# Attention with mixed heads and two feed-forward layers: the values' product reads in storage order and writes PSUM in token order, and the first loads are reordered

## The chip, the cores and the metric

One Trainium2 chip, one core of it. The metric is device time in microseconds (us) of one execution. Five engines run their own instruction streams: TensorE (PE in the rows, with PEld for its weight loads), VectorE (DVE), ScalarE (ACT), GpSimd (POOL) and SyncE (SP), which here only issues DMAs. PSUM is where TensorE writes, SBUF is the working memory.

## What is computed

The inputs are q, k, v of shape (4, 12, 448, 64) in float32, two 12x12 matrices that mix the heads before and after the softmax, and two feed-forward layers of width 2048 on 1792 tokens of width 768, whose weights are float64.

```
scores = scale * q @ k^T                     # per batch and head, 448 x 448
scores = einsum('bhij,hg->bgij', scores, w_pre)
attn   = exp(scores - max) / (sum + 1e-9)
attn   = einsum('bhij,hg->bgij', attn, w_post)
x      = (attn @ v) as 1792 x 768
h = x @ w_in;   x = (h * cos(h)) @ w_out
h = x @ w_in2;  x = (relu(h) ** 2) @ w_out2
```

## The kernel before

The attention is made in 4 batches of 4 chunks of query rows (11, 12, 12 and 10 blocks of 10 rows each). For each chunk and each of six pairs of heads, `scores_ops` makes the products q k^T (L647), an engine copies them from PSUM to a tile `sh` (L655, L657), and SP moves each half with a DMA into a tile `t` that holds all 12 heads of a query row beside each other (L661). The loads of the next batch (`load_ops`, L515, and `value_loads`, L546) are laid out so that `turn_ops` (L570) can transpose q and k on TensorE.

For each pair of blocks, `pair_ops` mixes the heads on TensorE (L701, tile `m`), takes the row maximum (L709), exponentials (L717), the inverse sums, and then mixes the heads again on TensorE with the inverse sums in the moving operand (L747, tile `po`). `mixed` copies the result to `at` (L775, L777). In `at` the columns of one head are stored as (block, m), with five m to a block.

At the end of a chunk `value_ops` (L819) multiplies by v. Its two loops (L836, 128 rows and 64 columns of the array for each product, and L846, 64 rows and 64 columns) accumulate over the keys in one PSUM tile `av`. All operands are float32, and each such product stands in the trace as two records. The moving operand is read as

```
rhs=ao[:, 3 * r + jc, g, :w].rearrange("p (k m) -> p m k", m=HI)
```

so five runs of 10 to 12 elements, each with a step of five elements (20 bytes), and PSUM is written contiguously. ScalarE and VectorE then split the sums into two float16 parts in `x` (L859, L863).

Beside the attention, the sixteen pieces of w_in are loaded (L319), scaled, split into float16 parts and stored (L1810). After it the two layers run (L1145, L1245, L1541, L1738), with the weights of w_out, w_in2 and w_out2 being prepared beside the products.

The order on each engine is written before the run by the class `Plan` (L27): each operation has costs, dependences, buffers to acquire and a key. A model of the engines takes, at each moment, the ready operation with the smallest key. `KEYS` (L175) are the numbers that set these keys. What the planner holds as a cost or a dependence makes an order only; on the chip, waits come from data and buffers alone. All DMAs but those of the mixing matrices are issued by SP, in one order.

At the start SP issues the 24 loads of the first q and k (L533), the moves of the first chunk's scores (L661), the eight loads of v (L558), three pieces of w_in (L319) and the next batch's q (L535).

Of the kernel before, what the change touches and what calls it, by code (L numbers as in the profile page):

```python
# [9 lines left out]
F32 = mybir.dt.float32  # L10
# [16 lines left out]
class Plan:  # L27
# [3 lines left out]

    LAT, DMA_START, DMA_END = 170.0, 650.0, 1000.0
    ENGINES = ("PE", "ACT", "DVE", "POOL", "SP")
# [6 lines left out]

    def op(self, eng, cost, key, fn, deps=(), acq=(), rel=(), dma=None, seq=(), alone=False):
        o = {
            "alts": eng if isinstance(eng, dict) else {eng: cost},
            "key": (key, len(self.ops)), "fn": fn, "acq": tuple(acq), "rel": tuple(rel),
            "out": [], "next": [], "need": 0, "done": False, "n": len(self.ops), "dma": dma, "slot": {},
            "alone": alone,
        }
        for d in deps:
            if d is not None:
                self.after(o, d)  # L50
        for d in seq:
            d["next"].append(o)
            o["need"] += 1
        self.ops.append(o)
        return o

    def after(self, o, d):
# [3 lines left out]
    def run(self):  # L61
# [17 lines left out]
        while events:  # L79
# [12 lines left out]
            for e in self.ENGINES:  # L92
# [46 lines left out]
def tile_talking_heads_attention_two_ffn(  # L139
# [35 lines left out]
    KEYS = {  # L175
        "pm": (-2.47, -3.04, -3.36, -2.62),
        "po": (0.64, 0.12, 1.81, 1.95),
        "av": (-859.93, -0.46, -80.63, -319.88),
        "s": (-36.83, -2.97, -2.5, -3.27),
        "sd": (7.77, 0.78, 0.72, 0.91),  # L180
        "ld": (416.51, 281.47, 277.67),
        "t": (-175.97, -746.81, -11.1),
        "td": (16.48, -868.16, -740.81),
        "vl": (87.51, -100.51, -140.48),
        "v": (968.18, 285.48, -1312.57),
        "vd": (765.72, 172.63, -541.73),
        "t0": (306.0, -893.18),
        "f0": (-785.12, 21.82),
        "v0": (572.08, -1105.53),
        "w": (-55.5, 136.26, 197.7, 8.83, 82.8, -49.29, -83.67, 192.84, 126.4, 466.75, 452.07, -639.94, 926.33, 128.86, 649.7, 476.96),  # L190
        "w2": (102.69, -3359458.07),
        "wo": (2.01, 8.53),
    }
    SHB, EB, GB = 3, 5, 3
    SLOTS = (1, 2, 3, 1, 2, 3, 2, 3, 2, 3, 2, 3, 3, 3, 0, 0)
    WARM = (22, 6)
# [113 lines left out]
    def word_ops(src, rows, cols, nm, key, place, deps, acq=()):  # L310
# [43 lines left out]

        ld = add("SP", 475, key, load, deps, acq=acq, dma=3.85 * n)
        o = add({"POOL": 40 + 1.04 * n, "ACT": 190 + 0.83 * n}, 0, key, expo, [ld])
# [35 lines left out]
    def attention(r1, actx):  # L392
# [122 lines left out]
        def load_ops(b, key, step, seq=()):  # L515

            last, done = seq, []
            for hp in range(0, NP, step):
                outs = []
                for nm, src in (("q", q), ("k", k)):  # L520
                    parts = [(z, c) for z in range(2) for c in (range(NC4) if step > 1 else [None])]
                    for z, c in parts:
                        def go(e, nm=nm, src=src, z=z, c=c, hp=hp):
                            if (b, nm) not in raw:
                                raw[b, nm] = new_raw((b, nm)).rearrange(
                                    "p (h c x) -> p h c x", h=NP, c=NC4
                                )
                            to = raw[b, nm][:CP, hp : hp + step, :, 64 * z : 64 * z + 64]
                            hs = src[b, 2 * hp + z : 2 * (hp + step) : 2].rearrange(
                                "h (p c) d -> p h c d", c=NC4  # L530
                            )
                            if c is None:
                                SP.dma_start(out=to[:, 0], in_=hs[:, 0])  # L533
                            else:
                                SP.dma_start(out=to[:, :, c], in_=hs[:, :, c])  # L535
# [5 lines left out]
                        last = [o]  # L541
                        outs.append(o)
                done += [outs] * step
            return done, last

        def value_loads(b, key, seq=()):  # L546
# [9 lines left out]
            for p0, jc, t0, c, n in parts:  # L556
# [4 lines left out]

                o = add("SP", 570, key, go, acq=[] if outs else ["v"], dma=13.5 * n, seq=last)
                last = [o]
# [6 lines left out]
        def turn_ops(b, keys, loads):  # L570

            outs, last = [], None
            for hp in range(NP):
# [14 lines left out]
                def keep(e, hp=hp, box=box):  # L588
# [9 lines left out]
                outs.append(add(  # L598
                    {"ACT": 950, "DVE": 1060}, 0, keys[hp], keep, [last], rel=[("m", last)], alone=True
                ))  # L600
# [35 lines left out]
        def scores_ops(b, ch, hp, key, turned, before):  # L636
# [22 lines left out]
            def move(z):  # L659
# [6 lines left out]
                return go  # L666

            o = add(
                "PE", 760, key, mm, [turned[hp], before],
                acq=["m"] + (["t"] if hp == 0 else []), rel=[f"qk{hp}"] if ch == 3 else [],  # L670
            )
            l = add(
                {"ACT": 950, "DVE": 1060}, 0, key, copy, [o], acq=["sh"], rel=[("m", o)], alone=True
            )
            return o, [
                add("SP", 850, key, move(z), [l], rel=["sh"] * z, dma=10 * m) for z in range(2)
            ]
# [7 lines left out]
        def pair_ops(st, moved, before_pm, before_po):  # L685
# [84 lines left out]
            def mixed(e):  # L770
# [31 lines left out]
            )  # L802
            o = add("DVE", 1090 if n == 2 else 580, s + 0.1, row_max, [pm], alone=True)
            ex = add("ACT", 830 * n, s + 0.2, exps, [o], acq=["e"], rel=[("m", pm), "pm"])
            rc = add({"DVE": 80, "POOL": 230}, 0, s + 0.3, guard, [ex])
            rc = add("DVE", 140, s + 0.3, recip, [rc], alone=True)
            rc = add({"DVE": 190, "POOL": 350}, 0, s + 0.4, mixer, [rc, w4], acq=["g"])
            po = add(
# [3 lines left out]
            low = add(  # L812
                {"ACT": 890, "DVE": 1000} if n == 2 else {"ACT": 950, "DVE": 800}, 0,
                s + KEYS["po"][b] + 0.1, mixed, [po], acq=["at"] if st.blk[0] == 0 else [],
# [4 lines left out]
        def value_ops(b, ch, key, lows, vready, before):  # L819
# [4 lines left out]
            def mm(e):  # L824
# [36 lines left out]
            def lo(e):  # L861
# [6 lines left out]
            o = add(  # L868
                "PE", 4900, key, mm, [before] + lows + vready[0] + x_free[b], acq=["m"],
                rel=["at"] + (["v"] if ch == 3 else []),  # L870
            )
            h = add("ACT", 850, key + 0.1, hi, [o] + vready[1])
            x_fin[b].append(add("DVE", 1100, key + 0.15, lo, [h], rel=[("m", o)], alone=True))
            return o


        def spaced(nm, n):
            return [KEYS[nm][0] + KEYS[nm][1] * i for i in range(n)]
# [916 lines left out]
    for f in range(NF):  # L1795
# [9 lines left out]
        def write(w, o, n, f=f, i=i, box=box):  # L1805
# [8 lines left out]
            o = halves(w, get, o, n, key)  # L1814
            return add("SP", 475, key, store, [o], dma=1060, rel=[] if i else ["raw"])

# [45 lines left out]
```

## Time and profile before

| | us |
|---|---|
| median of 3 runs | 1453.8 |
| lowest and highest | 1444.34, 1456.33 |
| the profiled execution, device time | 1451.96 |
| its span in the trace | 1449.9 |
| attention, until the last values' product | 0 to 518 |
| TensorE busy over the span | 1336.8 |

The span runs from the first to the last instruction; 2.1 us of the device time lie outside it. Busy time counts an instruction as long as its record, and records of matmuls overlap.

### The profile page before, as it was taken

How to read it: one execution, taken by the hardware profiler on the slowest of the kernel's cores; microseconds unless marked ns; L12 is line 12 of the kernel's file. 1: busy time of each engine (PE TensorE's matmuls, PEld its weight loads, DVE VectorE, ACT ScalarE, POOL GpSimd, SP SyncE). 2: the span in 40 equal slices, each digit the busy share in tenths (PEclk: the TensorE clock that was granted, in tenths of full speed). 3: DMA queues.
4: the chain of work that ended last, by engine and by line, in shares of the span. 5: the costliest groups of instructions: out<-in, count | busy, mean ns of one | idle time of the engine just before them, and what ended most of it. 6: DMA issues, size and time to landing. Idle time of an engine off the chain costs nothing.

```text
span 1449.9 us, 35787 instructions
## 1 busy us (share of the span) xinstructions
PE 1336.8 (92%) x15255; PEld 880.1 (61%) x15255; DVE 895.8 (62%) x1647; ACT 677.3 (47%) x1271; POOL 387.2 (27%) x436
## 2 busy tenths in 40 slices
PE   7589999989989899999799999879699999999998
PEld 3266666656757664554354555435586976986965
DVE  3667767655466559979958977986873460361520
ACT  2556556564455447655425534653561440450620
POOL 3122201100012136435314524351332240140300
PEclk8799999999999999999999999989899999999999
DMA  8974595474374363122222231556871540441501
GB/s 172 209 210 143 176 190 177 152 165 122 99 170 151 143 176 86 50 81 83 82 82 83 97 124 64 145 194 191 291 263 46 174 149 22 157 166 43 193 17 28
DMA packets 190239, 194.39 MB, mean 134 GB/s; under 512 B 74764, under 2 KB 173696, under 8 KB 189056
## 3 DMA queue, kind: packets, MB, share of 16 engines
q1 hardware_dynamic: 189984, 192.09, 45.7%
q8 instruction: 120, 1.97, 0.6%
q14 instruction: 39, 0.32, 0.1%
q0 software_dynamic: 96, 0.01, 0.0%
HBM read 124.27 MB, written 29.10 MB: 106 GB/s over the span
## 4 chain that ended last, share of the span: by engine, by line
PE 66%; DVE 14%; DMA 6%; issue 5%; ACT 5%; SPq 3%; POOL 2%; ACTq 0%; DVEq 0%; POOLq 0%
PE o L1738 15%; PE y L1245 9%; PE h_b L1541 9%; PE av L836 8%; PE h_a L1145 6%; PE po L747 5%; PE m L701 4%; PE hx_b L1541 4%; PE s L647 4%; DMA t<-sh 3%; DVE raw L337 1%; PE av L846 1%; DVE raw L343 1%; DVE raw L263 1%; DMA raw<-in_moe_w_out 1%
## 5 line engine op out<-in xcount | busy, mean ns | idle before, releaser
L1145 PE MATMUL h_a<-x,win 128*128 128x448 f16 x1152 | 228.7, 359 | 5.1 <-DVE eout L236 2.6
L1245 PE MATMUL y<-g,wout 128*128 128x448 f16 x1152 | 225.5, 355 | 0.6 <-POOL wout L1050 0.6
L1541 PEld LDWEIGHTS <-win 128*128 128x128 f16 x2016 | 196.4, 99 | 12.4 <-issue 9.1
L1738 PE MATMUL o<-wout,g 128*128 128x384 f16 x1152 | 188.8, 326 | 0.0
L1145 PEld LDWEIGHTS <-win 128*128 128x128 f16 x1152 | 114.6, 100 | 113.3 <-issue 13.8
L1245 PEld LDWEIGHTS <-wout 128*128 128x128 f16 x1152 | 113.2, 99 | 107.1 <-issue 5.0
L1738 PEld LDWEIGHTS <-g 128*128 128x128 f16 x1152 | 112.7, 98 | 73.2
L709 DVE TENSOR_REDUCE mx<-m 128x2 f32<-128x896 f32 (+1 forms) x92 | 97.4, 1063 | 63.5 <-PE m L701 59.3
L1541 PE MATMUL h_b<-win 128*128 128x224 f16 x1152 | 124.5, 263 | 7.2 <-DVE win L1566 6.7
L747 PEld LDWEIGHTS po<-g,e 64*64 64x64 f32 x5040 | 92.1, 140 | 59.9 <-issue 40.0
L836 PEld LDWEIGHTS av<-at,v 128*64 128x64 f32 x2304 | 120.8, 155 | 10.2 <-ACT at L775 6.5
L836 PE MATMUL av<-at,v 128*64 128x60 f32 (+2 forms) x2304 | 124.6, 285 | 1.1 <-ACT at L775 0.8
L717 ACT ACTIVATE e<-m,mx 128x448 f32<-128x448 f32 x180 | 111.7, 631 | 16.4 <-DVE mx L709 10.5
L747 PE MATMUL po<-g,e 64*64 64x60 f32 x5040 | 98.4, 225 | 19.6 <-issue 10.4
L1754 DVE SCALAR_TENSOR_TENSOR ob<-o,cols,raw 128x384 f32<-128x384 f32 x28 | 17.3, 616 | 151.5 <-PE o L1738 151.5
L647 PE MATMUL s<-qk 64*120 64x448 f32 (+2 forms) x384 | 94.4, 591 | 9.9 <-ACT sh L655 4.7
L701 PE MATMUL m<-t,kpre 64*64 64x448 f32 x704 | 92.4, 600 | 9.8 <-ACT sh L655 5.9
L1566 DVE TENSOR_TENSOR win<-h_b,win 128x224 f32<-128x224 f32 x128 | 49.0, 390 | 75.9 <-PE h_b L1541 55.9
L1209 POOL TENSOR_TENSOR u<-u,k 128x448 f32<-128x448 f32 x43 | 59.9, 1403 | 88.9 <-DVE k L1204 88.6
L1710 POOL TENSOR_TENSOR r<-r 128x448 f32<-128x448 f32 x29 | 28.6, 985 | 203.6 <-ACT r L1585 203.6
L775 ACT ACTIVATE at<-po 128x840 f32<-128x840 f32 (+2 forms) x57 | 50.9, 899 | 62.4 <-PE po L747 61.9
L657 DVE COPY sh<-s 120x896 f32<-120x896 f32 (+2 forms) x44 | 47.7, 1086 | 42.0 <-PE s L647 33.3
(250 smaller groups left out, 1986.3 us busy)
## 6 DMA issues: line engine op xcount, KB each, us to landing
win<-wp SPq DMA_DIRECT2D x32, 768.0 KB
raw<-in_moe_w_out SPq DMA_DIRECT2D x21, 1024.0 KB
t<-sh SPq DMA_DIRECT2D x96, 210.0 KB
win<-wp SPq DMA_DIRECT2D x32, 576.0 KB
raw<-in_moe_w_in SPq DMA_DIRECT2D x16, 768.0 KB
x<-in_moe_w_in SPq DMA_DIRECT2D x14, 768.0 KB
wp<-raw SPq DMA_DIRECT2D x8, 1344.0 KB
t<-sh SPq DMA_DIRECT2D x48, 192.5 KB
```

The costliest lines, as they stand in the source:

```text
L647: PE.matmul(ps[:m, z, :S], lhsT=qk[r, hp, 0, i0 : i0 + m], rhs=qk[r, hp, 1], start=True, stop=True,)
L701: PE.matmul(st.ps[64 * x : 64 * x + 64, r, :S], lhsT=km[rows, 64 * r : 64 * r + 64], rhs=t[rows, st.blk[x]], start=True, stop=True,)
L709: DVE.tensor_reduce(st.mx[:, :n], st.ps[:, :n, :S], axis=AX.X, op=ALU.max, negate=True)
L717: ACT.activation(st.e[:, x], st.ps[:, x, :S], AF.Exp, bias=st.mx[:, x : x + 1], accum_out=st.sm[:, x : x + 1],)
L747: PE.matmul(ps[64 * c : 64 * c + 64, bank_, at_ : at_ + W], lhsT=st.e[64 * rows : 64 * rows + 64, r, 64 * jt : 64 * jt + 64], rhs=st.g[64 ...
L775: ACT.activation(to, x, AF.Copy)
L836: PE.matmul(out(gp, x, r), lhsT=v32[:, g, jc * D : (jc + 1) * D], rhs=ao[:, 3 * r + jc, g, :w].rearrange("p (k m) -> p m k", m=HI), start= ...
L1145: PE.matmul(hb[nm, x], lhsT=t_["win"][:, x, wh, c, :], rhs=xt[b][:, c, xh], start=(c == 0 and wh == 0 and xh == 0), stop=(c == NCC - 1 and ...
L1209: (POOL if e == "POOL" else DVE).tensor_tensor(box["u"], box["u"], box["k"], op=ALU.subtract)
L1245: PE.matmul(box["ps"][:, :S], lhsT=t_["wo1"][m // 3][:, wh, f, (m % 3) * P : (m % 3 + 1) * P], rhs=t_["g"][:, f, gh], start=(f == 0 and wh ...
L1541: PE.matmul(box[at], lhsT=wt[:, k % 4, wh, c, :], rhs=y(c, xh), start=(first and c == 0 and wh == 0 and xh == 0), stop=(c == HC - 1 and wh ...
L1738: PE.matmul(box["ps"][:, :HD], lhsT=(t_["g"][:, f, gh, t0 : t0 + P] if t0 + P <= S else rest()[:, f, gh]), rhs=t_["wo2"][:, 6 * hf : 6 * h ...
```

## The change

1. In `value_ops` both products read the moving operand contiguously and write PSUM through the view that swaps the two inner dimensions, so that PSUM holds the same as before.
2. Where the loads are made pair by pair (the first batch alone), k is issued by ScalarE's queue and q by SP's.
3. The first batch's transposes and the first chunk's scores get keys of -2000 on; the loads of v and of all pieces of w_in follow the issue of the first chunk's last move in the planner.
4. Loads that the planner calls `bulk` are held back in its model while the modelled DMA backlog is over 1500 ns.
5. The first chunk's scores are copied to buffers of the pool of the exponentials (five) and not to `sh` (three).
6. Several costs in the model, and all `KEYS`, have other values, so that the whole order is written anew.

```diff
+    def follow(self, o, d):
+        d["next"].append(o)
+        o["need"] += 1
...
-                    if all(self.room[r] > 0 for r in o["acq"]):
+                    if o["bulk"] and dma_free > t + self.BACKLOG:
+                        push(dma_free - self.BACKLOG, "go", None)
+                        passed.append(k)
+                    elif all(self.room[r] > 0 for r in o["acq"]):
                         found = o
...
+                            by = ACT if e == "ACT" else SP
                             if c is None:
-                                SP.dma_start(out=to[:, 0], in_=hs[:, 0])
+                                by.dma_start(out=to[:, 0], in_=hs[:, 0])
...
+                        by = "ACT" if step == 1 and nm == "k" else "SP"
                         o = add(
-                            "SP", 570, key, go, acq=["raw"] if hp == 0 and (z, c) == parts[0] else [],
-                            dma=3000 * step / NP / len(parts), seq=last,
+                            by, 660, key, go, acq=["raw"] if hp == 0 and (z, c) == parts[0] else [],
+                            dma=7400 * step / NP / len(parts), seq=last.get(by, seq), bulk=b > 0,
...
-                sh = box["sh"] = shp.tile([P, 2, S], F32, tag="sh", name=f"sh{b}_{ch}_{hp}")
+                pool, tag = (shp, "sh") if b + ch else (ep, "e")
+                sh = box["sh"] = pool.tile([P, 2, S], F32, tag=tag, name=f"sh{b}_{ch}_{hp}")
...
-                    return ps[64 * x : 64 * x + 64, r, gp * w : (gp + 1) * w]
+                    return ps[64 * x : 64 * x + 64, r, gp * w : (gp + 1) * w].rearrange(
+                        "p (m k) -> p k m", m=HI
+                    )
...
-                                    rhs=ao[:, 3 * r + jc, g, :w].rearrange("p (k m) -> p m k", m=HI),
+                                    rhs=ao[:, 3 * r + jc, g, :w],
...
-                                rhs=ao[h, 6, g, :w].rearrange("p (k m) -> p m k", m=HI),
+                                rhs=ao[h, 6, g, :w],
...
-        turned[0] = turn_ops(0, spaced("t0", NP), loads)
-        vloads = value_loads(0, NEG + 5, last)
-        vready[0] = values_prep_ops(0, vloads, spaced("v0", 9), wready)
+        turned[0] = turn_ops(0, [-2000 + hp for hp in range(NP)], loads)
         for hp in range(NP):
-            sc, mv = scores_ops(0, 0, hp, KEYS["f0"][0] + KEYS["f0"][1] * hp, turned[0], sc)
+            sc, mv = scores_ops(0, 0, hp, -2000 + hp, turned[0], sc)
             moved.setdefault((0, 0), []).extend(mv)
         mv = moved[0, 0][-1]
-        for f in range(NF):
-            if not SLOTS[f]:
-                plan.after(pieces[f]["load"], mv)
+        vloads = value_loads(0, NEG + 5, [mv])
+        vready[0] = values_prep_ops(0, vloads, spaced("v0", 9), wready)
+        for f in range(EARLY, NF):
+            plan.follow(pieces[f]["load"], mv)
```

## Rows read from the trace of the kernel before

**Rows 1.** Page, part 4: the chain that ended last, its lines' shares of the span.
```profile
PE o L1738 15%; PE y L1245 9%; PE h_b L1541 9%; PE av L836 8%; PE h_a L1145 6%; PE po L747 5%; PE m L701 4%; PE hx_b L1541 4%; PE s L647 4%; DMA t<-sh 3%; DVE raw L337 1%; PE av L846 1%; DVE raw L343 1%; DVE raw L263 1%; DMA raw<-in_moe_w_out 1%
```

**Rows 2.** Stretches: from:to, length, busy of PE, PEld, DVE, ACT, POOL, PEclk, DMA share, GB/s.
```profile
0.00:49.00 49.00, 28.71 (x130) 14.35 (x134) 15.46 (x35) 17.70 (x24) 13.53 (x18) 0.77 0.90 185
49.00:100.00 51.00, 39.22 (x696) 23.99 (x699) 33.06 (x65) 26.24 (x56) 9.13 (x19) 0.82 0.89 219
100.00:518.00 418.00, 389.19 (x8694) 275.30 (x8686) 259.36 (x470) 229.84 (x492) 62.11 (x147) 0.99 0.58 156
518.00:1450.00 932.00, 879.63 (x5757) 566.49 (x5755) 587.93 (x1081) 403.50 (x700) 302.44 (x252) 0.98 0.36 117
```

**Rows 3.** Stretches, whole span, of L836 and then of L846 alone: PE busy, PEld busy.
```profile
0.00:1450.00 1450.00, 124.56 (x2304) 120.81 (x2304) 0.97 0.46 134
...
0.00:1450.00 1450.00, 23.44 (x768) 19.77 (x768) 0.97 0.46 134
```

**Rows 4.** Timeline of PE, three moments: start us, us, line, shapes, records.
```profile
64.97 1.04 PE L747 MATMUL po<-g,e 64*64 64x60 f32 x56 [0.24 <-ACT at L775]
...
116.23 8.24 PE L836 MATMUL av<-at,v 128*64 128x60 f32 x144
124.40 1.54 PE L846 MATMUL av<-at,v 64*64 64x60 f32 x48
...
182.26 1.33 PE L846 MATMUL av<-at,v 64*64 64x50 f32 x48
```

**Rows 5.** Groups by line and shape on PE: busy us, mean ns of one.
```profile
L747 PE MATMUL po<-g,e 64*64 64x60 f32 x5040 | 98.4, 225 | 19.6 <-issue 10.4 <-ACT at L775 3.6 <-ACT e L717 1.5
...
L836 PE MATMUL av<-at,v 128*64 128x60 f32 x1152 | 65.9, 292 | 0.8 <-ACT at L775 0.8
...
L846 PE MATMUL av<-at,v 64*64 64x60 f32 x384 | 12.4, 289 | 0.0
...
L846 PE MATMUL av<-at,v 64*64 64x50 f32 x192 | 5.3, 270 | 0.0
```

**Rows 6.** Timeline of all engines, 0 to 49 us; SPq is SP's queue issuing.
```profile
0.74 1.41 SPq L533 DMA_DIRECT2D raw0q<-in_q  x2
...
23.10 1.28 SPq L533 DMA_DIRECT2D raw0k<-in_k  x2
23.18 0.66 PEld L580 LDWEIGHTS tr<-ident,raw0k 112*128 112x128 f32 x4 [6.29 <-DMA raw0k<-in_k]
...
24.43 6.66 SPq L558 DMA_DIRECT2D v<-in_v  x7
...
33.63 0.64 SPq L319 DMA_DIRECT2D x<-in_moe_w_in  x1
...
40.25 7.70 SPq L535 DMA_DIRECT2D raw1q<-in_q  x2
...
48.90 3.26 PE L701 MATMUL m<-t,kpre 64*64 64x448 f32 x16 [0.51 <-ACT sh L655]
```

**Rows 7.** The chain in order of time, 0 to 100 us: start, us, what.
```profile
37.20 10.63 DMA t<-sh
...
61.13 5.50 DMA t<-sh
...
90.73 8.22 DMA x<-in_moe_w_in
```

**Rows 8.** Waits, 0 to 49 us: us in total, times, longest.
```profile
ACT sh L655 <- DMA t<-sh: 10.9, 4, 5.8
```

**Rows 9.** DMA, 0 to 49 us: the sum, then issues with the size of each.
```profile
DMA packets 21323, 9.04 MB, mean 185 GB/s; under 512 B 17975, under 2 KB 21322, under 8 KB 21322
...
t<-sh SPq DMA_DIRECT2D x12, 192.5 KB
x<-in_moe_w_in SPq DMA_DIRECT2D x3, 768.0 KB
raw0q<-in_q SPq DMA_DIRECT2D x12, 112.0 KB
```

More of the change, by code (lines that the diff above doesn't have):

```diff
@@ L39, in __init__, with op @@
         self.log = []
-    def op(self, eng, cost, key, fn, deps=(), acq=(), rel=(), dma=None, seq=(), alone=False):
+    def op(self, eng, cost, key, fn, deps=(), acq=(), rel=(), dma=None, seq=(), alone=False, bulk=False):
         o = {
@@ L45, in op @@
             "out": [], "next": [], "need": 0, "done": False, "n": len(self.ops), "dma": dma, "slot": {},
-            "alone": alone,
+            "alone": alone, "bulk": bulk,
         }
@@ L51, in op @@
         for d in seq:
-            d["next"].append(o)
-            o["need"] += 1
+            self.follow(o, d)
         self.ops.append(o)
         return o
+    def follow(self, o, d):
+        d["next"].append(o)
+        o["need"] += 1
     def after(self, o, d):
@@ L175, in tile_talking_heads_attention_two_ffn @@
     KEYS = {
[L176 to L192, printed above, removed]
+        "pm": (-8.08, -122.35, -5.92, -8.53),
+        "po": (-5.11, -61.13, 136.66, 944.76),
+        "av": (-333.85, 1020.12, -3.47, -348.91),
+        "s": (-287.63, -5.41, -786.11, -378.76),
+        "sd": (243.9, 0.09, 148.35, 56.37),
+        "ld": (-297.31, -97.57, 207.68),
+        "t": (405.87, 577.23, -6.74),
+        "td": (925.58, -209.79, 2.13),
+        "vl": (507.51, 1111.52, -323.39),
+        "v": (341.3, -444.25, 436.67),
+        "vd": (19.33, -672.95, 307.06),
+        "v0": (873.15, 1837.63),
+        "w": (-6.6, -82.01, 9.81, -224.56, -237.15, -763.62, -204.32, 584.75, 298.55, -304.98, -694.63, 1055.93, -756.97, -861.44, 133.67, 1443.56),
+        "w2": (42.41, -912103.99),
+        "wo": (-0.7, 4.14),
     }
     SHB, EB, GB = 3, 5, 3
+    EARLY = 0
     SLOTS = (1, 2, 3, 1, 2, 3, 2, 3, 2, 3, 2, 3, 3, 3, 0, 0)
@@ L353, in squares @@
             )
-        ld = add("SP", 475, key, load, deps, acq=acq, dma=3.85 * n)
+        ld = add("SP", 475, key, load, deps, acq=acq, dma=3.85 * n, bulk=True)
         o = add({"POOL": 40 + 1.04 * n, "ACT": 190 + 0.83 * n}, 0, key, expo, [ld])
@@ L515, in load_ops @@
         def load_ops(b, key, step, seq=()):
-            last, done = seq, []
+            last, done = {}, []
             for hp in range(0, NP, step):
@@ L560, in go @@
                     )
-                o = add("SP", 570, key, go, acq=[] if outs else ["v"], dma=13.5 * n, seq=last)
+                o = add("SP", 660, key, go, acq=[] if outs else ["v"], dma=16.5 * n, seq=last, bulk=True)
                 last = [o]
@@ L598, in turn_ops @@
                 outs.append(add(
-                    {"ACT": 950, "DVE": 1060}, 0, keys[hp], keep, [last], rel=[("m", last)], alone=True
+                    {"ACT": 830, "DVE": 1000}, 0, keys[hp], keep, [last], rel=[("m", last)], alone=True
                 ))
@@ L666, in move @@
                 return go
+            sh = "sh" if b + ch else "e"
             o = add(
                 "PE", 760, key, mm, [turned[hp], before],
-                acq=["m"] + (["t"] if hp == 0 else []), rel=[f"qk{hp}"] if ch == 3 else [],
+                acq=["m", sh] + (["t"] if hp == 0 else []), rel=[f"qk{hp}"] if ch == 3 else [],
             )
             l = add(
-                {"ACT": 950, "DVE": 1060}, 0, key, copy, [o], acq=["sh"], rel=[("m", o)], alone=True
+                {"ACT": 830, "DVE": 1000}, 0, key, copy, [o], rel=[("m", o)], alone=True
             )
             return o, [
-                add("SP", 850, key, move(z), [l], rel=["sh"] * z, dma=10 * m) for z in range(2)
+                add("SP", 850, key, move(z), [l], rel=[sh] * z, dma=10 * m) for z in range(2)
             ]
@@ L802, in pair_ops @@
             )
-            o = add("DVE", 1090 if n == 2 else 580, s + 0.1, row_max, [pm], alone=True)
-            ex = add("ACT", 830 * n, s + 0.2, exps, [o], acq=["e"], rel=[("m", pm), "pm"])
-            rc = add({"DVE": 80, "POOL": 230}, 0, s + 0.3, guard, [ex])
+            o = add("DVE", 1000 if n == 2 else 540, s + 0.1, row_max, [pm], alone=True)
+            ex = add("ACT", 610 * n, s + 0.2, exps, [o], acq=["e"], rel=[("m", pm), "pm"])
+            rc = add({"DVE": 80, "POOL": 190}, 0, s + 0.3, guard, [ex])
             rc = add("DVE", 140, s + 0.3, recip, [rc], alone=True)
-            rc = add({"DVE": 190, "POOL": 350}, 0, s + 0.4, mixer, [rc, w4], acq=["g"])
+            rc = add({"DVE": 190, "POOL": 340}, 0, s + 0.4, mixer, [rc, w4], acq=["g"])
             po = add(
@@ L872, in value_ops @@
             h = add("ACT", 850, key + 0.1, hi, [o] + vready[1])
-            x_fin[b].append(add("DVE", 1100, key + 0.15, lo, [h], rel=[("m", o)], alone=True))
+            x_fin[b].append(add("DVE", 980, key + 0.15, lo, [h], rel=[("m", o)], alone=True))
             return o
@@ L1814, in write @@
             o = halves(w, get, o, n, key)
-            return add("SP", 475, key, store, [o], dma=1060, rel=[] if i else ["raw"])
+            return add("SP", 475, key, store, [o], dma=1060, rel=[] if i else ["raw"], bulk=True)
         key = KEYS["w"][f]
```

12 lines of the change are left out of this document (6 added, 6 removed).

## The prediction, made before the result was known

> **What bounds the kernel now.** I read the chain that ended last first, then a table of stretches, then single operations on TensorE, and the start last.
>
> The chain lies on TensorE for most of the span; the values' product has 8% and 1% of it (its two loops, L836 and L846), so some 130 us, and the moves t<-sh have 3% [rows 1]. The stretches tell two regimes apart [rows 2]. From 100 to 518 us, the attention after its start, TensorE is busy for 389.2 of 418 us at a granted clock of 0.99 (nearly all at 2.4 GHz), while VectorE has 259.4, ScalarE 229.8 and the DMA engines a share of 0.58: TensorE sets the pace, and its idle time is 28.8 us or 7%. In the first 100 us it is the other way round: TensorE is busy for 28.7 of 49 and 39.2 of 51 us at clocks of 0.77 and 0.82, and the DMA share is 0.90 and 0.89. There transfers and their order set the pace. After 518 us TensorE is busy for 879.6 of 932 us, and no named edit touches that part; only the keys do.
>
> **The values' product.** L836 and L846 have 124.6 + 23.4 = 148.0 us of busy time [rows 3]. Whether a contiguous read makes them shorter is read from the spacing of records. I take the length of a run of records, less the length of its last one, over the number of steps. L846 at 60 columns: (1.54 - 0.289) / 47 = 26.6 ns. The head mixing L747 has the same tile shape (64x64, so four tiles of the array at once), the same 60 float32 columns and a weight tile of the same size, but it reads contiguously: (1.04 - 0.225) / 55 = 14.8 ns [rows 4, 5]. So the strided read costs a factor of 1.80. That it isn't the weight load or a fixed cost of issue shows at 50 columns: (1.33 - 0.270) / 47 = 22.6 ns, less by 1.18 where the columns are fewer by 1.20 [rows 4, 5]. L836 at 60 columns has (8.24 - 0.292) / 143 = 55.6 ns, twice 27.8: two tiles at once where L846 has four, and the same slowness in each [rows 4, 5]. If the read alone is slow, the 148.0 us become 148.0 / 1.80 = 82, so 66 us of TensorE's work go.
>
> The new write has no row: in the kernel before, every product of L836, L846 and L747 writes contiguously. After the change, five neighbouring columns land nb words (10 to 12, so 40 to 48 bytes) apart. Its cost is bounded by nothing (gain 66) and, taking the strided read as the nearest row, by the same 26.6 ns (gain 0); a write dearer than that read is a rival below, and a gain beyond 66 is excluded, since the contiguous row is the floor. I take nothing: L747 is nearest in shape and data path, and a float32 column takes several passes of the array (14.8 x 4 = 59 ns for 60 columns in one tile, so 2.4 cycles of 2.4 GHz for each column of a record), which leaves a write more than two cycles for each column.
>
> Against that stands a rule. The Trainium skill, "PSUM — Partial Sum Buffer", section "Specifications (TRN2)", says that PSUM works in lines of 8 bytes and that an access pattern which isn't contiguous slows matmuls significantly. By that rule the slowness only moves from the read to the write, and the sum would be that of the first rival. No row here shows a strided write, so the trace neither agrees nor disagrees.
>
> **How much of 66 us reaches the end.** Fifteen of the sixteen products lie after 100 us, so about 62 us of it come out of the 389.2. TensorE then has 328 us of work there. VectorE's 259 and ScalarE's 230 us stay, and in a stretch of some 365 us they are busy for 71% and 63% (62% and 55% now); the DMA share goes from 0.58 to about 0.67 [rows 2]. TensorE is still the longest, but its waits on copies, maxima and moves grow. With the idle share as now, 7%, the stretch is 328 / 0.93 = 353 (gain 65); with 15% it is 386 (gain 32). I take 11%: 368.5, a gain of 49. The next to be late is VectorE, with the row maximum, the copies and the preparation of w_in in one queue.
>
> **The start.** SP issues two loads in 1.28 us [rows 6], so the 24 first loads cost it 15.4 us; half of them go to ScalarE, 7.7 us on each. But the time is the transfers': 9.04 MB pass in 49 us, 185 GB/s [rows 9]. The first chunk needs of these 24 loads of 112 KB and 12 moves of 192.5 KB [rows 9], 2.75 + 2.37 = 5.12 MB. Between them go v, three pieces of 768 KB of w_in and the next q, which keep SP itself waiting (7.70 us for two issues at 40.25). The last loads of k are only issued at 23.10 us, and the transpose behind them waited 6.29 us [rows 6]. The first mixing product starts at 48.90 us [rows 6]; the chain before it is a move that took 10.63 us [rows 7]. Four copies to `sh` waited 10.9 us for moves to land, as three buffers are all there is [rows 8]; with five others for the first chunk, this wait goes for those copies. 5.12 MB at 185 GB/s are 28 us; if the last move still takes 10.63 us more, 39. So the first mixing product comes 10 to 21 us earlier.
>
> What was moved back isn't gone: 3.9 MB at 219 GB/s are 18 us of transfers, put into a stretch with a share of 0.89 [rows 2], and v is due by the end of the first chunk. If they delay the second chunk's moves as the chain shows now (5.50 and 8.22 us at 61 and 91 us [rows 7]), the gain is eaten. If SP's order spreads them past 100 us, where the share is 0.58, it stays. Taken: 14, ends 0 and 21.
>
> Smaller parts: ScalarE's 12 issues take 7.7 us of its queue, with the copies of transposed q and k behind them. ScalarE has 17.7 us of work in the first 49 [rows 2], so I cost it at nothing; if an issue met a full queue as SP's at 40.25 did, 3.85 us each. The first exponentials share five buffers with the moves, but the mixing product ahead of them waits for the same moves: nothing. The planner's holding back of bulk loads and its costs add no wait on the chip; they are an order. The new keys also reorder the preparation of weights beside the layers. That part has 52 us of idle TensorE [rows 2]; I take 0 and 10 either way, a fifth of it, as an estimate.
>
> **Sum.** 1452.0 (the profiled execution, of which 2.1 lie outside the span; the median is 1453.8) - 49 - 14 = 1389. Its own ends: 1452 - 65 - 21 - 10 = 1356 at the utmost, and 1452 - 32 - 0 + 10 = 1430; as these don't fall together, 1364 to 1414.
>
> **Rivals.**
> 1. The strided write takes what the strided read took. Then the product stays at 148 us and only the start gains: 1452 - 14 = 1438. For it: the read has shown that steps cost a factor of 1.80 on one memory. Against it: the two cycles for each column above. By the skill's rule named before, this is the result.
> 2. The write is dearer than the read was, and the kernel becomes slower. Four-tile spacing s prices the product: (2304 x 2 + 768) x s, so each ns is 5.4 us. With the start's gain of 14 the kernel loses from 26.6 + 2.6 = 29.2 ns on. At 38 ns (the strided read and, on top, the step of 11.8 ns that strides cost now) it is 1452 + 62 - 14 = 1500. For it: accumulating products read PSUM as well as write it. Against: nothing in the rows is this slow.
> 3. The work goes but waits take its place: the idle share rises to 15% and the delayed loads eat the start's gain. 1452 - 33 = 1419. For it: from 49 to 100 us TensorE is idle for 23% where the DMA share is 0.89. Against it: the share after 100 us has room.
>
> **How the numbers follow.** The forecast 0.61, rival 1 0.16, rival 2 0.07, rival 3 0.14, anything else 0.02. The three runs of before lie 12 us apart, so 1% is about what tells a change from none: 1439 to 1468. Faster: 0.61 + 0.14 + half of rival 1, whose 1438 stands on the bound, 0.08, so 0.83. Slower: 0.07 and 0.01 of the rest. Same: 0.09. The range takes in the forecast's ends, rival 3 and the nearer half of rival 1: 1358 to 1440; outside it stay rival 2, the upper half of rival 1 and some of the forecast's lower end.
>
> **What would show it.** A product at 60 columns of 144 records in about 4.5 us and 48 records in about 0.9, against 8.24 and 1.54, shows the read's part; still 8.2 shows rival 1, over 9 rival 2. The last values' product near 455 us in place of 518 shows the sum; TensorE's idle share after the start shows the 11%. The first mixing product at 28 to 39 us shows the start's first half, and how soon the first product with v follows shows whether the loads moved back bite. I am wrong if strided writes cost, if the second chunk waits for its moves behind v and w_in, or if the layers' part moves by more than 10 us.

## The result, and the profile after

The changed kernel takes 1400.5 us (median of 4 runs, 1396.8 to 1407.1), 0.964 of the kernel before (95% interval 0.957 to 0.971). That is 51 us less than the 1452 of its profiled execution and 55 less than the median of its 4 runs, 1455; 63 were forecast. The profiled execution took 1402.1 us, of which the span is 1400.4.

The first view after it is the table of stretches. The columns are those of [rows 2]; the third stretch ends at 470, shortly before the first layer's products start at 475.5.

```profile
0.00:49.00 49.00, 42.45 (x499) 22.65 (x503) 26.97 (x48) 18.32 (x34) 14.17 (x25) 0.93 0.78 168
49.00:100.00 51.00, 36.05 (x758) 20.06 (x752) 21.93 (x44) 25.90 (x58) 2.65 (x10) 0.90 0.76 180
100.00:470.00 370.00, 316.57 (x7905) 208.42 (x7901) 250.80 (x469) 233.39 (x488) 59.94 (x133) 0.95 0.64 175
470.00:1400.00 930.00, 884.56 (x6116) 571.46 (x6116) 591.88 (x1083) 407.02 (x706) 311.25 (x257) 0.98 0.38 121
```

From 100 us to the first product of the layers, at 475.5 us here and 518.1 before, the time is now 43 us less, and from there to the end of the span 7 us less (925 and 932). The last values' product, which the prediction put near 455 us, ends at 488 (516 before), since the new order puts it behind the layers' start. In the 370 us of the third row TensorE has 317 us of work, in [rows 2] 389 of 418, but it is idle for 53 us, 14%, where it was for 29, 7%. The granted clock fell from 0.99 to 0.95. VectorE and ScalarE did what they did before (251 and 233 us).

The timeline of TensorE, at two moments, shows the product:

```profile
326.17 4.42 PE L847 MATMUL av<-at,v 128*64 128x60 f32 x144
...
101.71 0.92 PE L857 MATMUL av<-at,v 64*64 64x60 f32 x48
102.45 0.39 PE L756 MATMUL po<-g,e 64*64 64x60 f32 x10
106.44 1.44 PE L756 MATMUL po<-g,e 64*64 64x60 f32 x43 [3.59 <-issue]
```

With 223 ns for the last record (the mean of this group), (4.42 - 0.223) / 143 = 29.3 ns from record to record, where [rows 4] gave 55.6; in the second loop it is (0.92 - 0.224) / 47 = 14.8, where it was 26.6. The last line is the surprise of this case: TensorE stops for 3.59 us in the middle of one head mixing, after 10 of its 56 records. The profile shows nothing that those records wait for, and calls such a stop "issue". These are all such waits of the changed kernel over 1 us on TensorE's matmuls (total, times, longest):

```profile
PE po L756 <- issue: 24.6, 15, 3.7
...
PE av L857 <- issue: 6.1, 3, 4.6
...
PE av L847 <- issue: 5.7, 6, 1.8
...
PE m L710 <- issue: 4.0, 1, 4.0
```

Before, the head mixing had 10.4 us of them [rows 5] and the product next to none. What happens in such a stop shows in the DMA view of 102.84 to 106.44 us, the 3.59 us stop (first the busy share of the DMA engines in 40 slices, then the packets by queue):

```profile
DMA  9999999999999999999999999975231211111111
...
q1 hardware_dynamic: 903, 0.89, 77.4%
q8 instruction: 1, 0.02, 2.0%
```

One packet of 16 KB passes on the queue named instruction, and the profile names nothing else that releases TensorE in that time. The page counts 120 such packets, 1.97 MB, over the span, for some 30,750 instructions of TensorE (15,255 weight loads, as many matmuls, 242 waits). That makes one packet for 256 instructions, and the experiments bear it out: run 7, with 2304 instructions of TensorE fewer, has 111 packets, and run 6, with 3840 fewer, has 105.

The trace's records show how the stops go with the packets. Between 100 us and the attention's end TensorE stops 45 times for over 0.3 us, that is, it has neither a matmul nor a weight load under way. After 23 of these stops, 34.9 us in all, it starts again 1.15 to 1.8 us after the end of such a packet. The 66 packets of that time, with 0.65 us each, cover 11% of it, so by chance some 5 stops would. In the kernel before, 9 of 20 stops are of this kind, with 11.7 us. So on this chip waits don't come from data and buffers alone, as was said ahead of the prediction.

The start in the changed kernel, from the timeline of all engines (ACTq is ScalarE's queue):

```profile
0.75 12.63 ACTq L539 DMA_DIRECT2D raw0k<-in_k  x12
0.75 13.21 SPq L539 DMA_DIRECT2D raw0q<-in_q  x12
...
15.65 25.50 SPq L669 DMA_DIRECT2D t<-sh  x22
...
33.77 1.73 PE L710 MATMUL m<-t,kpre 64*64 64x448 f32 x16
...
41.19 2.21 SPq L565 DMA_DIRECT2D v<-in_v  x3
```

The first mixing product comes at 33.8 us (48.9 in [rows 6]), in the forecast's bounds of 28 to 39. All 22 moves that SP issues, ten of the second chunk's among them, go ahead of v, and v then passes in small portions.

### The profile page after: what moved, and what is told of

Its sections match the earlier page's. It is cut to its first block, busy times and chain, and to the rows that moved or that the text cites. A ratio compares the mean times of both kernels' runs of the same rounds, so it can differ in the third digit from the quotient of the medians.

```text
span 1400.4 us, 35812 instructions
## 1 busy us (share of the span) xinstructions
PE 1279.6 (91%) x15255; PEld 822.6 (59%) x15255; DVE 891.6 (64%) x1643; ACT 684.6 (49%) x1286; POOL 388.0 (28%) x425
## 3 DMA queue, kind: packets, MB, share of 16 engines
q8 instruction: 120, 1.97, 0.6%
## 4 chain that ended last, share of the span: by engine, by line
PE 69%; DVE 17%; issue 6%; ACT 4%; DMA 2%; POOL 1%; SPq 0%; DVEq 0%; ACTq 0%; POOLq 0%
PE o L1748 15%; PE y L1255 12%; PE h_a L1155 9%; PE h_b L1551 8%; PE s L654 5%; PE po L756 5%; PE av L847 5%; PE hx_b L1551 3%; PE m L710 3%; DVE raw L342 2%; PE tr L587 1%; DVE raw L348 1%; DVE mx L718 1%; ACT e L726 1%; DVE raw L268 1%
## 5 line engine op out<-in xcount | busy, mean ns | idle before, releaser
L1551 PEld LDWEIGHTS <-win 128*128 128x128 f16 x2016 | 193.3, 98 | 8.2 <-issue 6.9
L1155 PEld LDWEIGHTS <-win 128*128 128x128 f16 x1152 | 114.4, 100 | 113.5 <-issue 14.2
L756 PE MATMUL po<-g,e 64*64 64x60 f32 x5040 | 98.2, 228 | 31.1 <-issue 24.6
L654 PE MATMUL s<-qk 64*120 64x448 f32 (+2 forms) x384 | 99.6, 613 | 8.1 <-DVE qk L599 2.5
L710 PE MATMUL m<-t,kpre 64*64 64x448 f32 x704 | 87.3, 580 | 12.4 <-ACT e L726 4.8
L847 PEld LDWEIGHTS av<-at,v 128*64 128x64 f32 x2304 | 71.3, 141 | 20.3 <-ACT at L784 7.7
L847 PE MATMUL av<-at,v 128*64 128x60 f32 (+2 forms) x2304 | 74.3, 225 | 8.1 <-issue 5.7
L663 ACT ACTIVATE sh<-s 120x896 f32<-120x896 f32 (+2 forms) x62 | 56.3, 916 | 42.5 <-PE s L654 35.3
L1720 POOL TENSOR_TENSOR r<-r 128x448 f32<-128x448 f32 x25 | 24.1, 963 | 185.4 <-ACT r L1595 185.4
L733 POOL TENSOR_SCALAR rs<-sm 128x2 f32<-128x2 f32 (+1 forms) x71 | 17.0, 240 | 202.9 <-ACT e L726 195.7
```

Source lines behind the costliest of these rows:

```text
L654: PE.matmul(ps[:m, z, :S], lhsT=qk[r, hp, 0, i0 : i0 + m], rhs=qk[r, hp, 1], start=True, stop=True,)
L663: ACT.activation(sh[:m], box["ps"][:m, :, :S], AF.Copy)
L710: PE.matmul(st.ps[64 * x : 64 * x + 64, r, :S], lhsT=km[rows, 64 * r : 64 * r + 64], rhs=t[rows, st.blk[x]], start=True, stop=True,)
L756: PE.matmul(ps[64 * c : 64 * c + 64, bank_, at_ : at_ + W], lhsT=st.e[64 * rows : 64 * rows + 64, r, 64 * jt : 64 * jt + 64], rhs=st.g[64 ...
L847: PE.matmul(out(gp, x, r), lhsT=v32[:, g, jc * D : (jc + 1) * D], rhs=ao[:, 3 * r + jc, g, :w], start=(gp + jc == 0), stop=False, skip_gro ...
L1155: PE.matmul(hb[nm, x], lhsT=t_["win"][:, x, wh, c, :], rhs=xt[b][:, c, xh], start=(c == 0 and wh == 0 and xh == 0), stop=(c == NCC - 1 and ...
```

## The experiments

Each row of times is a median; ratios are to the kernel before on the same chip, with 95% intervals. "Unexplained" is the sum, in us, of the waits on issue of TensorE's matmuls from 100 us to the first product of the layers, and "idle" the whole of TensorE's idle time there. In the new order the last values' product comes after that point, so a row is compared with rows of the same order.

| kernel | us | ratio | idle | unexplained |
|---|---|---|---|---|
| before | 1452 to 1455 | 1 | 28.8 | 10.6 |
| changed | 1400.5 | 0.964 (0.957 to 0.971) | 55.2 | 33.3 |
| 1 product alone | 1417.2 | 0.977 (0.974 to 0.980) | 39.8 | 19.7 |
| 2 changed, old product | 1437.8 | 0.991 (0.988 to 0.993) | 39.2 | 17.1 |
| 3 start alone | 1467.4 | 1.012 (1.009 to 1.015) | | |
| 4 changed, plain write | 1400.8 | 0.966 (0.963 to 0.969) | | |
| 5 changed, second loop left out | 1381.2 | 0.951 (0.948 to 0.954) | 51.5 | 24.0 |
| 6 as 5, half the records | 1372.7 | 0.945 (0.943 to 0.948) | 50.0 | 16.5 |
| 7 changed, half the records | 1374.3 | 0.946 (0.943 to 0.948) | 42.6 | 20.4 |
| 8 changed, nothing held back | 1462.2 | 1.008 (1.005 to 1.010) | | |
| 9 start alone, with holding back | 1494.2 | 1.027 (1.024 to 1.030) | | |
| 10 before, half the records | 1399.7 | 0.963 (0.960 to 0.966) | 31.1 | 4.7 |
| 11 changed, k issued by SP | 1428.7 | 0.984 (0.980 to 0.987) | | |

**1. The product's edit alone, in the old order.**

```diff
-                    return ps[64 * x : 64 * x + 64, r, gp * w : (gp + 1) * w]
+                    return ps[64 * x : 64 * x + 64, r, gp * w : (gp + 1) * w].rearrange(
+                        "p (m k) -> p k m", m=HI
+                    )
...
-                                    rhs=ao[:, 3 * r + jc, g, :w].rearrange("p (k m) -> p m k", m=HI),
+                                    rhs=ao[:, 3 * r + jc, g, :w],
...
-                                rhs=ao[h, 6, g, :w].rearrange("p (k m) -> p m k", m=HI),
+                                rhs=ao[h, 6, g, :w],
```

> The kernel before with the product's edit alone, in the order of before. If the read's step is the whole cost and TensorE sets the pace: about 29 ns from record to record at 60 columns (55.6 before), 66 us less of TensorE's work, and 1403 us (49 less). Rival, the supply of instructions: the product is as fast, but TensorE's idle time that no wait explains (10.6 us of it before the two groups po and av, 41 in the changed kernel) grows to over 25 us, and the time stays near 1415 to 1425. Rival, the gain of the changed kernel is the start's and the keys': 1440 or more.

1417.2 us, 35 less. The stretches of the two loops over the whole span, as in [rows 3], then the stretch from 100 us to the layers, then its waits on issue:

```profile
0.00:1410.00 1410.00, 72.98 (x2304) 70.62 (x2304) 0.96 0.47 138
...
0.00:1410.00 1410.00, 15.51 (x768) 13.08 (x768) 0.96 0.47 138
...
100.00:477.00 377.00, 337.23 (x8650) 222.50 (x8643) 258.05 (x467) 230.18 (x492) 62.97 (x147) 0.97 0.64 173
...
PE po L747 <- issue: 11.2, 8, 2.8
PE av L838 <- issue: 4.8, 3, 2.7
PE av L848 <- issue: 3.7, 3, 1.6
```

The 148.0 us of the product are 88.5, so 59.5 us went and not 66. The timeline shows why:

```profile
335.02 4.42 PE L838 MATMUL av<-at,v 128*64 128x60 f32 x144
...
375.27 4.41 PE L838 MATMUL av<-at,v 128*64 128x50 f32 x144
379.61 0.92 PE L848 MATMUL av<-at,v 64*64 64x50 f32 x48
```

A chunk of 50 columns takes as long as one of 60. In the kernel before it took less, 6.96 and 1.33 us for 8.24 and 1.54 [rows 4]; its line for 6.96 is

```profile
175.38 6.96 PE L836 MATMUL av<-at,v 128*64 128x50 f32 x144
```

Read contiguously, then, 50 to 60 columns cost the same time for each record, 29.3 ns with two tiles and 14.8 with four, and the factor of 1.80 that was read at 60 columns is smaller at 50 and 55.

The stretch has lost 52.0 us of TensorE's work, and its idle time grew by 11.0 us; 9.1 of these are waits on issue. The forecast's part of this edit, 49, is 35. That is the time that the supply theory gave, but it asked for over 25 us of unexplained waits, and there are 19.7. VectorE has 258 us of 377 and didn't become the one that is late.

**2. The changed kernel with the old product.** The same lines the other way round.

> The changed kernel with the product as before (strided read, contiguous write), its order and its start kept. By the forecast's sum 1438: only the start's 14 us are left. If the new keys alone are worth much, 1425 or less. If the new order was only good for a fast product, 1450 or more, though the first mixing product still comes near 34 us.

1437.8 us: the sum's value to the microsecond. So the product is worth 37 us in the new order (35 in the old), and the rest of the change 14. The stretch from 100 us has 39.2 us of idle time here:

```profile
100.00:503.00 403.00, 363.80 (x8079) 255.96 (x8077) 252.78 (x476) 235.12 (x490) 60.42 (x134) 0.98 0.59 161
...
PE po L756 <- issue: 14.3, 11, 3.8
```

With the fast product the idle time is 55.2, 16.0 more, and the waits on issue are 33.3 in place of 17.1, 16.2 more. In this order, too, what grew is the waits on issue, and not waits for a neighbour.

**3. The start's edits alone.**

```diff
+                        by = "ACT" if step == 1 and nm == "k" else "SP"
                         o = add(
-                            "SP", 570, key, go, acq=["raw"] if hp == 0 and (z, c) == parts[0] else [],
+                            by, 570, key, go, acq=["raw"] if hp == 0 and (z, c) == parts[0] else [],
...
+                pool, tag = (shp, "sh") if b + ch else (ep, "e")
+                sh = box["sh"] = pool.tile([P, 2, S], F32, tag=tag, name=f"sh{b}_{ch}_{hp}")
...
-        turned[0] = turn_ops(0, spaced("t0", NP), loads)
+        turned[0] = turn_ops(0, [-2000 + hp for hp in range(NP)], loads)
...
+        vloads = value_loads(0, NEG + 5, [mv])
...
+            plan.follow(pieces[f]["load"], mv)
```

> The kernel before with the edits of the start alone: k issued by ScalarE, the first chunk's transposes, scores and moves ahead of v and w_in, its scores in five buffers; product, costs and all other keys as before. By the forecast 1438, with the first mixing product 10 to 21 us earlier than 48.9. Rival, the loads moved back collide with the second chunk's moves: the first product with v comes no more than 5 us earlier than at 85.5, and the time is 1450 or more.

1467.4 us, 16 slower: the forecast's 14 us aren't the start's. The chain in order of time, then SP's queue:

```profile
63.26 7.76 PE av L843 x141
...
108.27 8.16 PE av L843 x144
```

```profile
13.69 14.24 SPq L667 DMA_DIRECT2D t<-sh  x12
27.98 8.89 SPq L563 DMA_DIRECT2D v<-in_v  x8
36.91 1.14 SPq L322 DMA_DIRECT2D x<-in_moe_w_in  x1
38.16 5.28 SPq L667 DMA_DIRECT2D t<-sh  x6
...
45.18 15.78 SPq L539 DMA_DIRECT2D raw1q<-in_q  x8
```

The first product starts at 63.3 us and not at 85.5, a gain of 22. The second starts at 108.3 (116.2 in [rows 4]), and by the third nothing is left of it (148.2 and 147.6 us, from the records). Neither expectation is met as it stands: the time is the rival's, but the first product isn't late.

Only twelve moves stand ahead of v; the second chunk's are between v, w_in and the next q, which hold SP for 15.78 us. That looks like the collision that the prediction named, but the trace doesn't show that it ate the gain. Between the starts of the first two products TensorE's longest waits are 3.1 us for VectorE's and 2.6 for ScalarE's work on w_in, and only 1.5 for a DMA; its mean granted clock from 63 to 108 us is 0.85, where from 85.5 to 116.2 in the kernel before it was 1.00.

As the two kernels are level at the third product, the 16 us are lost behind it. TensorE's largest waits there are for the preparation of the weights, which the same planner put in another order. These three had 4.8, 3.3 and 0 us in the kernel before:

```profile
PE n_in L275 <- DVE k L1223: 13.2, 2, 10.2
PE n_out L304 <- ACT raw L354: 9.5, 2, 7.4
PE n_in L275 <- DVE stp L1365: 9.4, 3, 6.4
```

**4. A contiguous write.**

```diff
-                    return ps[64 * x : 64 * x + 64, r, gp * w : (gp + 1) * w].rearrange(
-                        "p (m k) -> p k m", m=HI
-                    )
+                    return ps[64 * x : 64 * x + 64, r, gp * w : (gp + 1) * w]
```

> The changed kernel with contiguous read and contiguous write: the tokens of a chunk come out in another order, so the output differs. If a strided write costs nothing: 29.3 ns from record to record as in the changed kernel, and the time within 4 us of it (1400). If the write's step costs something that the read's did not show: 26 ns or less, and 5 us or more off the time.

1400.8 us, and on TensorE's timeline:

```profile
322.18 4.42 PE L845 MATMUL av<-at,v 128*64 128x60 f32 x144
326.53 0.93 PE L855 MATMUL av<-at,v 64*64 64x60 f32 x48
```

4.42 and 0.93 us against 4.42 and 0.92: the strided write costs nothing that can be seen. As the contiguous product takes the same time at 50 and at 60 columns (run 1), a cost of the write that is hidden under that time isn't excluded.

**5 and 6. Half the records, the second loop left out in both.** Run 5 is the changed kernel without its second loop; run 6 writes the first loop so:

```diff
+                def out(gp, x):
+                    at_ = gp % 3 * 2 * w
+                    return ps[64 * x : 64 * x + 64, gp // 3, at_ : at_ + 2 * w]
+
+                def whole(gp, jc):
+                    for x in range(2):
+                        g = 2 * gp + x
+                        PE.matmul(
+                            out(gp, x).rearrange("p (r m k) -> p r k m", r=2, m=HI),
+                            lhsT=v32[:, g, jc * D : (jc + 1) * D],
+                            rhs=ao[:, jc:6:3, g, :w].rearrange("p r (k m) -> p r k m", m=HI),
+                            start=(gp % 3 + jc == 0), stop=(jc == 2), skip_group_check=True,
+                        )
...
+                        whole(gp, jc)
```

> The changed kernel without the second loop of the values' product: the last 64 keys of each row are left out, so the output differs. A control for the next run: 768 records and some 16 us of TensorE's busy time go, 1385 to 1395 by both theories.

> The control with the first loop written as half as many products of 120 columns (both halves of the rows of a chunk in one product, three head pairs to a PSUM bank), the last 64 keys left out as there: the same columns through the array, 1152 records and as many weight loads fewer. Theory, the supply of instructions: the idle time of TensorE that no wait explains falls by 10 us or more, and the time is 10 to 25 us below the control. Rival, the neighbours (VectorE, ScalarE, moves) hold TensorE up: such idle time only changes its name, and the time is within 6 us of the control, that is no more than what the products themselves lose in overheads (about 5 us).

1381.2 and 1372.7 us. Run 5 is 4 us below what either theory gave. The 8.5 us between them fall between the two: the waits on issue fell from 24.0 to 16.5, but the idle time only from 51.5 to 50.0, so that other waits took most of their place. The rest of the 4 us by which the stretch is shorter is TensorE's work, 2.4 us: the records of `av` are busy for 10.1 us less (60.3 to 50.2), but those of `m` for 4.8 more (73.9 to 78.7). With this pair alone the supply theory isn't settled.

```profile
100.00:451.00 351.00, 299.46 (x7242) 195.62 (x7233) 251.18 (x475) 233.93 (x489) 58.25 (x133) 0.96 0.66 182
```

```profile
100.00:447.00 347.00, 297.03 (x6421) 186.10 (x6419) 253.71 (x479) 235.16 (x490) 58.89 (x134) 0.95 0.68 183
```

**7 and 10. A whole kernel with half the records, in the new order and in the old.** The first loop is that of run 6. The second takes all 128 rows and weights with zeros in one half, and follows the first for each pair of heads:

```diff
-        v32 = atc.tile([P, H, 4 * D], F32, name="v32")
+        v32 = atc.tile([P, H, 5 * D], F32, name="v32")
...
+            POOL.memset(v32[64:, :, 3 * D : 4 * D], 0.0)
+            POOL.memset(v32[:64, :, 4 * D :], 0.0)
...
-            parts.append((64, 3, CP - 64, 3, 64))
+            parts.append((64, 4, CP - 64, 3, 64))
...
+                                out(gp, x)[:, r * w : (r + 1) * w].rearrange(
+                                    "p (m k) -> p k m", m=HI
+                                ),
+                                lhsT=v32[:, g, (3 + r) * D : (4 + r) * D], rhs=ao[:, 6, g, :w],
```

> A whole kernel with the halved first loop; the second loop uses all 128 rows with zeros in the weights' other half, as its two row halves may not write one bank at once. It costs 48 records at two tiles in place of four, 0.7 us for each of 16 products, 11 us. By the supply theory 1380 to 1395, below the changed kernel; by the rival 1402 to 1412, above it.

> The halved product of e7 in the order of the kernel before, whose counterpart is e1 (1417): the supply theory tried in another order. TensorE's busy time with av falls by some 5 us and its unexplained waits by 5 to 10: 1400 to 1408. If e7's 26 us were an accident of that order: within 6 us of e1.

1374.3 and 1399.7 us: the best version of this study is 26 us below the changed kernel and below what either theory gave, and the same edit in the old order is 18 us below run 1. Run 7's stretch and its waits on issue, then run 10's:

```profile
100.00:447.00 347.00, 304.39 (x6959) 198.12 (x6955) 252.74 (x476) 234.87 (x490) 59.25 (x134) 0.97 0.67 185
...
PE po L758 <- issue: 16.9, 12, 2.9
```

```profile
100.00:463.00 363.00, 331.86 (x7531) 217.60 (x7522) 256.89 (x465) 227.81 (x490) 61.82 (x146) 0.97 0.62 172
...
PE po L749 <- issue: 3.6, 5, 2.0
```

The waits on issue fell by 12.9 us in the new order and by 15.0 in the old, the idle time by 12.6 and 8.7, and TensorE's work in these stretches by 15.5 and 5.4. The stops that end 1.15 to 1.8 us after an instruction packet went from 23 to 14 (34.9 to 20.6 us) and, from run 1 to run 10, from 17 to 7 (21.5 to 6.6). So in both orders the supply of instructions was a real part of what the forecast had missed. Part of the gain is another: a record of 120 columns costs less than two of 60.

```profile
233.78 0.79 PE L846 MATMUL av<-at,v 128*64 128x120 f32 x12
234.40 0.40 PE L859 MATMUL av<-at,v 128*64 128x60 f32 x8
```

With 268 ns for the last record, (0.79 - 0.268) / 11 = 47.5 ns, where two of 60 columns take 58.6. The second loop now takes (0.40 - 0.220) / 7 = 26 ns in place of 14.8. Together the records of `av` are busy for 6 us less over the span in run 7 (89 to 83) and 5 less in run 10 (87 to 82). The remaining work that went from run 7's stretch isn't the product's; its granted clock is 0.97 where the changed kernel has 0.95.

**8. Nothing held back in the planner.**

```diff
-    LAT, DMA_START, DMA_END, BACKLOG = 170.0, 650.0, 1000.0, 1500.0
+    LAT, DMA_START, DMA_END, BACKLOG = 170.0, 650.0, 1000.0, 1e9
```

> The changed kernel without the planner's holding back of bulk loads (the limit raised beyond any backlog); all else the same. If it is what keeps the loads moved back from eating the start's gain: the third chunk's product ends later than in the changed kernel (146.0 us) and the time is 1410 or more. If the other order of loads and the keys do that: within 6 us of 1400.

1462.2 us. The third product ends at 150.9 us (146.0 in the changed kernel), but most is lost later, to waits for moves and for the preparation of w_in:

```profile
PE n_in L306 <- ACT x L356: 19.7, 4, 9.5
PE m L710 <- DMA t<-sh: 15.6, 2, 8.1
```

**9. The start's edits with the holding back.** Run 3 with `bulk` and the loads' new costs in the planner (660 for an issue, 7400 and 16.5 for the transfers).

> The kernel before with the start's edits (as e3), the planner's holding back of bulk loads and the loads' new costs in its model; product, other costs and other keys as before. If the holding back is what makes the moved-back loads harmless: the third chunk's product ends by 145 us (157.9 in e3) and the time is 1440 or less (1467 in e3). If it is only one number among keys that fit each other: 1455 or more.

1494.2 us, slower than without it. The third product does end earlier, at 147.4 us where run 3 has 157.9, but what is gained there is lost later: the layers' first product starts at 526 us and not at 499. The holding back isn't a cure by itself; with the new `KEYS` it is part of a kernel that gains. TensorE's longest wait is now for moves:

```profile
PE m L711 <- DMA t<-sh: 14.8, 4, 5.0
```

**11. All first loads by SP.**

```diff
-                        by = "ACT" if step == 1 and nm == "k" else "SP"
+                        by = "SP"
```

> The changed kernel with all 24 first loads issued by SP again. If only the issue time is saved by ScalarE's queue, as transfers are the limit: the first mixing product within 3 us of 33.8, and a time within 6 us of 1400. If the second queue matters: first mixing product at 38 or later and 1406 or more.

1428.7 us. TensorE's timeline at the start:

```profile
32.27 0.98 PE L587 MATMUL tr<-ident,raw0k 112*128 112x112 f32 x4 [4.38 <-DMA raw0k<-in_k]
...
44.21 0.98 PE L710 MATMUL m<-t,kpre 64*64 64x448 f32 x8
```

The last k is transposed at 32.3 us, and the first mixing product comes at 44.2 and not at 33.8: SP has moves between the loads again. So without the second queue, and with the order that the planner then writes, the start loses 10 us. The whole time has that other order in it, too, and isn't all due to the queue.

## Why the prediction was right, and which of its terms were not

**The read and the write.** Right in mechanism, and in size at 60 columns. The spacing was forecast as 2 x 14.8 and 14.8 ns and is 29.3 and 14.8; the loops take 4.42 and 0.92 us for 4.5 and 0.9. Rivals 1 and 2 fall with run 4. The Trainium skill, "PSUM — Partial Sum Buffer", section "Specifications (TRN2)", says that an access pattern which isn't contiguous slows matmuls significantly; for float32 products of 60 columns that write each five neighbours 48 bytes apart the trace disagrees, 4.42 us with the steps and 4.42 without.

**The work.** Too large: 66 us were to go and 59.5 went (148.0 to 88.5, run 1). The whole product was divided by the factor of 1.80, which was read at 60 columns, but half of the chunks have 50 or 55, and read contiguously they take as long as those of 60. The prediction tested a fixed cost for each record on the strided rows alone (22.6 ns at 50 columns, 26.6 at 60); on contiguous rows its 2.4 cycles for each column don't hold. At 144 and 48 records for each chunk the product's runs go from some 146 us (9.7, 9.0 and 8.2 us at 60, 55 and 50 columns) to 85 (5.3 each), 61 us less, an estimate from the timelines; that is near what went.

**How much of it reaches the end.** 49 was taken, 35 (run 1) and 37 (run 2 against the changed kernel) were measured. In run 1 the guessed idle share, 11%, is what came (39.8 of 377 us); the stretch is longer than the forecast's 368.5 because 337 us of work are left there and not 328. That the share came out is luck, since the place was wrong: VectorE's queue was named as the next to be late, but 9.1 of the 11.0 us of added idle time are waits on issue. In the changed kernel the share is 15% (55.2 of 375), and waits on issue grew by as much as the idle time did over run 2, 16.2 and 16.0. Runs 7 and 10 bear this out by taking instructions away; run 6 alone would not have. With the idle time the granted clock fell, from a mean of 0.99 to 0.95. In the rows of two chunks of the changed kernel,

```profile
102.60:146.00 43.40, 31.20 (x655) 22.13 (x645) 27.94 (x52) 26.34 (x49) 8.31 (x12) 0.90 0.49 153
146.00:177.30 31.30, 27.99 (x558) 15.80 (x562) 23.21 (x46) 18.44 (x38) 6.24 (x11) 0.81 0.51 162
```

the first has two stops of 3.59 and 4.59 us, the second of them just ahead of its end at 146, and the chunk after it ran at a mean of 0.81, so over a third of it at 1.2 GHz. From 144 to 150 us, within that second stop and behind it, the granted clock is 0.50.

**The start and the keys.** The two terms, 14 and 0, have the right sum by luck (run 2: 14 less than before) and are both wrong. The start's edits alone cost 16 us (run 3): a gain of 22 is gone by the third product, as the third rival said, though the trace doesn't show that the moves are the reason, and then TensorE waits for the layers' weights, whose preparation the planner reordered. The new costs and keys with the holding back give 30 (run 2 against run 3). The step that failed is that the keys were costed at nothing, with 10 us either way: they decide whether the start's edits gain or lose, and run 8 shows that one number of the planner less is worth 62 us. That ScalarE's queue would only spread the issue time was wrong too, as far as run 11 tells: with the order that goes with it, it is worth 10 us of the start.

**What stays open.** How the 30 us divide between the new costs, the new keys and the holding back wasn't tried, as each of them only works with the others' values; nor was it settled why run 6 gained less than run 7, beyond that other waits took the place of those on issue. What sets the time of a contiguous record at 50 to 60 columns wasn't tried.

## What to carry to other kernels

Compare the spacing of records with that of a contiguous product of the same tile shape and columns before looking at anything else: a factor there says which operand's step to move. Read the factor at every width that the kernel has, as the fast product may not get faster with fewer columns. When a stream of small products becomes twice as fast, look for stops that no wait explains, in the middle of an operation, and count the instructions; fewer and longer products can then be worth more than fewer columns. An order found by search is one object: a sensible edit of the start, or one limit taken out, can cost more than it brings until the numbers around it are set anew.

## What the runs showed of the hardware

- TensorE stops for want of instructions: in the changed kernel 0.3 to 4.6 us at a time, ending 1.15 to 1.8 us after a 16 KB packet of the queue named instruction, one packet for 256 of its instructions (9 packets fewer for 2304 instructions fewer in run 7). These packets come at least 3.5 us apart in the changed kernel (3.3 in run 1), while 256 instructions of the product are used up in 3.75 us (29.3 ns for a weight load and a matmul) and those of the head mixing in 1.9 us (14.8). The five longest of these stops, 2.8 to 4.6 us, all began with the DMA engines 80% busy or more; whether bulk loads delay the packet was not tried by itself.
- Float32 products that read contiguously take the same time for each record at 50 and at 60 columns, 29.3 ns with two tiles and 14.8 with four (run 1); with two tiles, 120 columns take 47.5 ns (run 7).
- A step of 20 bytes in the float32 moving operand costs a factor of 1.8 to 1.9 at 60 columns, with four tiles and with two, and 1.5 to 1.6 at 50. A step of 48 bytes in the PSUM write of the same products at 60 columns costs nothing that shows (4.42 us in run 4 and in the changed kernel).
